# Which engine multiplies q's rows by 1/rms, in the six slots beside the first batch's MLP

## The chip, the cores and the metric

The kernel runs on one core of a Trainium2 chip. The core has a matrix engine (TensorE, PE in the profile, with its weight loads listed apart as PEld), three engines for element-wise work (VectorE = DVE, ScalarE = ACT, GpSimd = POOL), and SyncE (SP), whose queue here issues nearly all the DMAs. Every engine works its own instructions in order and waits on semaphores for the others. The metric is the device time of one execution in microseconds (us); the number quoted is the median of several executions.

## The reference

Attention with normalised q and k for 8 batches of 12 heads (448 positions, head width 64), followed by a two-layer MLP (768 to 2048 to 768) with the activation h - tanh(h):

```
q_n = q / sqrt(mean(q*q) + 1e-6) * g_q
k_n = k / sqrt(mean(k*k) + 1e-6) * g_k
attn = softmax(q_n @ k_n.T / sqrt(64))
x    = heads of (attn @ v) side by side          # (3584, 768)
h    = x @ w_in
out  = (h - tanh(h)) @ w_out
```

q, k, v are float32. The two weight matrices come as float64 and are rounded to float32 in the kernel.

## The kernel before

The attention is cut into 48 steps, one for each pair of heads of each batch (`NP` = 6 pairs, `NCH` = 4 chunks of rows, `D` = 64, `CP` = 112 rows of q in a chunk, `S` = 448). The program is written out as 51 slots, and the order of the calls in a slot is the order of the instructions on each engine: the schedule is by hand. Slots -3 to 5 (`first_slot`) hold attention alone and the first weights. Slots 6 to 11 (`early_slot`) hold attention of the second batch beside the MLP of the first; slots 12 on (`slot`) hold attention beside the MLP of the batch before. `run(gap)` puts a given amount of MLP matmuls at that place of the slot. In slots 6, 7 and 8 these are the matmuls of the first layer (line 669, 224 columns), in slots 9, 10 and 11 those of the second (line 834, 448 columns).

A step's q goes this way. Three slots ahead, `squares` (line 123) has ScalarE square q's rows into the tile `n`. `norm` (lines 133 to 135) sums them on VectorE and takes the power -1/2 on GpSimd, first for q (112x8 factors, one per row and head) and then for k. `norm_q` (line 401) multiplies q's rows by these factors, again into `n`; it is the last call of `early_slot`, after the last `run`. One slot on, `turn` (line 410) transposes k and `n` on TensorE into two PSUM banks (lines 415 and 419), and ScalarE copies them out (417, 423). There is one tile `n`, and two q tiles take turns.

The start of the next slot follows `norm_q` directly: `totals` (matmuls of line 572, whose VectorE reciprocal is line 577), then the first scores (499) with their exps on ScalarE (504). The PSUM banks named `sc` are five and go round in order: one for `totals`, four for the first scores, and `turn` takes the `totals` bank again and then the bank of the first exp.

Through slots -3 to 10 the weights are rounded. A piece is 768 KB of float64; one DMA or four bring it (lines 265, 269), then ScalarE makes two passes over it (71, 72), VectorE three (78, 79, 82, one piece behind ScalarE), and GpSimd adds the two parts (90). For all but the first eight pieces the raw data have three buffers (`w_raw`), and the next load waits on SP for the GpSimd add that frees one. Finished weights and their sums (324, 341 to 344) are written back to DRAM (332, 348), to be read again by the later batches (386, 388).

So the instructions ahead of and behind `norm_q` on VectorE in these slots are weight passes, their sums, and the additions of the MLP (725 to 739); on ScalarE the exps, the weight passes and the tanhs (705).

Of the kernel before, what the change touches and what calls it, by code (L numbers as in the profile page):

```python
# [20 lines left out]
NCH = 4  # L21
# [116 lines left out]
def bounded_path(tc, ctx, q, k, v, moe_w_in, moe_w_out, out, g_col, ident, ones, half_ones, neg_half, early):  # L138
# [17 lines left out]
    nc = tc.nc  # L156
# [3 lines left out]
    CP = S // NCH  # L160
    NP = H // 2
# [239 lines left out]
    def norm_q(s):  # L401
        rr, n = normed[s], early["n"]
        t = loaded.pop(("q", s))
        nc.vector.tensor_tensor(
            out=n.rearrange("p c h d -> p h c d"), in0=t,
            in1=rr[:CP, 1].rearrange("p (h c) -> p h c", h=2)[:, :, :, None].to_broadcast([CP, 2, NCH, D]),
            op=ALU.mult,
        )
# [470 lines left out]
    def first_slot(s):  # L879
# [21 lines left out]
        if has(s + 1):  # L901
            scores(s + 1, 2)
            add(s + 1)
            add_last(s + 1)
        norm_q(s + 3)
        if s == -3:
            early["g_col"]()
# [5 lines left out]
    def early_slot(s):  # L913
        gap = gap_ns(s)
        totals(s, sc_bank())
        if has(s + 1):
            scores(s + 1, 0)
            scores(s + 1, 1)
        if has(s + 2):
            load(s + 2, "v")  # L920
        run(gap)
        if has(s + 2):
            turn(s + 2, sc_bank(), sc_bank())
        if has(s + 3):
            squares(s + 3)
        if has(s + 4):
            load(s + 4, "qk")
        run(gap)
        if has(s + 1):
            scores(s + 1, KF)  # L930
        av = [sc_bank() for _ in range(2)]
        last_values(s, av)
        divide(s, values(s, av))
        if has(s + 1):
            scores(s + 1, 2)
        for work, n in ((add, 1), (add_last, 1), (norm, 3), (norm_q, 3)):
            run(gap / 2)
            if has(s + n):
                work(s + n)

    def slot(s):
# [50 lines left out]
        if ahead:  # L992
            norm_q(s + 3)
# [359 lines left out]
```

## Time and profile before

| | |
|---|---|
| Five runs | 1420.86 to 1427.71 us, median 1421.89 |
| The profiled execution | 1425.79 us, of which the span of the core is 1424.0 |
| Granted TensorE clock, mean | 0.989 |
| Busy share of the span | PE 97%, DVE 65%, POOL 37%, ACT 33% |

By stretches of the span (us, busy time of each engine; the six slots are about 85 to 292):

| Stretch | length | PE | DVE | ACT | POOL | clock |
|---|---|---|---|---|---|---|
| 92 to 123 | 31 | 30.37 | 30.41 | 16.58 | 18.47 | 1.00 |
| 123 to 152 | 29 | 29.00 | 26.85 | 15.58 | 16.69 | 1.00 |
| 152 to 184 | 32 | 26.13 | 25.34 | 14.95 | 13.23 | 0.84 |
| 184 to 200 | 16 | 13.70 | 15.79 | 8.67 | 12.50 | 0.98 |
| 200 to 235 | 35 | 35.00 | 29.82 | 17.02 | 18.14 | 0.96 |
| 235 to 270 | 35 | 33.81 | 31.17 | 9.59 | 15.90 | 0.95 |
| 270 to 300 | 30 | 30.00 | 19.04 | 7.98 | 6.07 | 1.00 |

A busy engine is one with an instruction begun and not ended; an instruction that is held up in the middle counts as busy all the while. Where PE is busy for less than the whole stretch it stands still for something. The clock is what TensorE was granted, 1.00 being full speed: a matmul of line 669 at half the clock takes twice as long.

### The profile page before, as it was taken

Reading aid. Unit: us, or ns where it says so; the run is one execution under the profiler, and the core shown is the slowest. Engines: PE = TensorE matmul, PEld = TensorE weight load, DVE = VectorE, ACT = ScalarE, POOL = GpSimd, SP = SyncE. Lnnn points to the kernel's source line nnn. Section 1 sums busy time; section 2 is a strip of 40 time slices with the busy share of each in tenths; the row PEclk is TensorE's granted clock in tenths of the full one; section 3 lists DMA queues with packets and bytes.
Section 4 is the critical chain, followed back from the end, with each engine's and each line's share of the span. In section 5 each row is a group of like instructions: output and inputs, shape, how many; then the busy total and the mean of one; then the engine's idle time right before and its main releaser. Section 6 shows DMA issues by size and latency. Waiting matters only on the chain.

```text
span 1424.0 us, 25566 instructions
## 1 busy us (share of the span) xinstructions
PE 1386.3 (97%) x9752; PEld 1165.8 (82%) x9752; DVE 928.0 (65%) x1571; ACT 466.8 (33%) x1070; POOL 523.8 (37%) x348
## 2 busy tenths in 40 slices
PE   6999899999999999999999999999999999999997
PEld 3568664478898799888989888987998888899997
DVE  3899879867655577567866578655875578632311
ACT  5765444233422333233332234223332333301100
POOL 4555555223521336214543145312462145401310
PEclk9999899999999999999999999999999999999999
DMA  8669788864565655665656666666556656365563
GB/s 181 165 190 245 235 247 204 219 192 149 169 169 154 166 164 176 173 171 161 178 152 186 160 162 180 172 157 167 160 174 175 171 161 179 123 180 174 187 192 95
DMA packets 355255, 249.72 MB, mean 175 GB/s; under 512 B 266484, under 2 KB 297396, under 8 KB 355124
## 3 DMA queue, kind: packets, MB, share of 16 engines
q1 hardware_dynamic: 355120, 248.00, 63.1%
q8 instruction: 79, 1.29, 0.4%
q14 instruction: 52, 0.43, 0.1%
q10 hardware_dynamic: 4, 0.00, 0.0%
HBM read 214.50 MB, written 33.42 MB: 174 GB/s over the span
## 4 chain that ended last, share of the span: by engine, by line
PE 86%; DVE 5%; DMA 3%; SPq 2%; ACT 2%; issue 1%; POOL 0%; ACTq 0%; DVEq 0%
PE mm L669 63%; PE sc L499 9%; PE sc L551 7%; PE mm L834 4%; PE sc L539 2%; SPq L265 1%; SPq L118 1%; DMA w_raw<-in_moe_w_out_dram 1%; DVE rs L577 1%; DVE w_out L82 1%; ACT sum_g L592 1%; DMA w_f<-w_in 0%; DMA gT<-in_moe_w_in_dram 0%; SPq L116 0%; DMA q_nat<-in_q_dram 0%
## 5 line engine op out<-in xcount | busy, mean ns | idle before, releaser
L669 PE MATMUL mm<-xT,w_f 128*128 128x224 f32 x1392 | 275.6, 354 | 0.0
L669 PEld LDWEIGHTS mm<-xT,w_f 128*128 128x128 f32 x1392 | 262.1, 190 | 9.1 <-issue 7.8
L669 PE MATMUL mm<-gT,w_f 128*128 128x224 f32 x1344 | 263.0, 354 | 0.0
L669 PEld LDWEIGHTS mm<-gT,w_f 128*128 128x128 f32 x1344 | 252.8, 190 | 11.4 <-issue 6.5
L457 POOL TENSOR_TENSOR rr_mine<-rr_mine,neg_half 128x28 f32<-128x28 f32 x30 | 145.1, 4835 | 251.8 <-DVE rr_mine L456 251.8
L669 PE MATMUL mm<-tt,w_f 128*128 128x224 f32 x1044 | 209.4, 354 | 5.4 <-DVE gT L706 5.4
L669 PEld LDWEIGHTS mm<-tt,w_f 128*128 128x128 f32 x1044 | 196.5, 190 | 11.4 <-DVE gT L706 7.5
L669 PE MATMUL mm<-tg,w_f 128*128 128x224 f32 x1008 | 197.7, 353 | 0.0
L706 POOL TENSOR_TENSOR gT<-s,th 128x448 f32<-128x448 f32 x96 | 115.7, 1215 | 212.7 <-ACT th L705 212.7
L669 PEld LDWEIGHTS mm<-tg,w_f 128*128 128x128 f32 x1008 | 190.6, 190 | 0.0
L499 PE MATMUL sc<-qT,kT 64*128 64x448 f32 (+1 forms) x960 | 167.4, 497 | 11.8 <-ACT p_last L504 8.3
L499 PEld LDWEIGHTS sc<-qT,kT 64*128 64x128 f32 (+1 forms) x960 | 70.1, 166 | 83.9 <-issue 60.4
L592 ACT COPY sum_g<-sum 32x14 f32<-32x14 f32 x280 | 56.3, 201 | 225.1 <-DVE sum L588 219.4
L613 DVE TENSOR_TENSOR xT<-sc,rs_T 64x224 f32<-64x224 f32 x140 | 54.4, 388 | 68.4 <-PE sc L551 66.4
L629 POOL TENSOR_TENSOR tt<-xT,tt 128x224 f32<-128x224 f32 x23 | 17.1, 744 | 222.0 <-DVE xT L613 221.9
L504 ACT ACTIVATE p<-sc 128x448 f32<-128x448 f32 x120 | 55.6, 550 | 97.9 <-PE sc L499 97.9
L705 ACT ACTIVATE th<-s 128x448 f32<-128x448 f32 x96 | 54.9, 578 | 85.0 <-DVE s L731 36.6
L135 POOL TENSOR_TENSOR rr<-rr,neg_half 112x8 f32<-112x8 f32 (+1 forms) x36 | 59.7, 1680 | 62.3 <-DVE rr L134 62.2
L551 PE MATMUL sc<-p,v_nat 128*32 128x224 f32 x1344 | 80.0, 355 | 0.0
L834 PE MATMUL mm<-gT,w_out 128*128 128x448 f32 x192 | 76.9, 557 | 0.0
L521 DVE TENSOR_TENSOR rows<-p 128x896 f32<-128x896 f32 x38 | 42.4, 1115 | 41.8 <-ACT p L504 41.7
L834 PEld LDWEIGHTS mm<-gT,w_out 128*128 128x128 f32 x192 | 36.9, 196 | 37.7 <-issue 36.3
(144 smaller groups left out, 1752.9 us busy)
## 6 DMA issues: line engine op xcount, KB each, us to landing
w_f<-w_in SPq DMA_DIRECT2D x196, 384.0 KB, 3.1
w_f<-w_out SPq DMA_DIRECT2D x147, 512.0 KB, 3.8
w_raw<-in_moe_w_out_dram SPq DMA_DIRECT2D x16, 768.0 KB, 5.1
out_dram<-th SPq DMA_DIRECT2D x192, 56.0 KB, 1.9
w_in<-w_out SPq DMA_DIRECT2D x21, 384.0 KB, 6.5
qk_nat<-in_q_dram SPq DMA_DIRECT2D x120, 56.0 KB, 2.4
qk_nat<-in_k_dram SPq DMA_DIRECT2D x120, 56.0 KB, 2.2
gT<-in_moe_w_in_dram SPq DMA_DIRECT2D x32, 192.0 KB, 4.1
```

The costliest lines, as they stand in the source:

```text
L135: nc.gpsimd.tensor_tensor(out=r, in0=r, in1=neg_half[:rows], op=ALU.pow)
L457: nc.gpsimd.tensor_tensor(out=mine, in0=mine, in1=neg_half[:, :1].to_broadcast([P, 2 * NJ]), op=ALU.pow)
L499: nc.tensor.matmul(tiles[h][i * keys : (i + 1) * keys, :n], lhsT=kT[r, c * P : c * P + keys], rhs=qT[r, i * n : (i + 1) * n], start=True, ...
L504: nc.scalar.activation(p[:, h, c if c < 2 else 0, :], tiles[h][:, :n], AF.Exp, scale=1.0 if rr is None else rr[:, 0, 2 * c + h : 2 * c + h ...
L521: nc.vector.tensor_tensor(out=t, in0=p[0], in1=p[1], op=ALU.add)
L551: nc.tensor.matmul(av[n][r : r + BL, :HS], lhsT=v_nat[:, h, c, m * BL : (m + 1) * BL], rhs=p[c][:, h, n * HS : (n + 1) * HS], start=False, ...
L592: nc.scalar.copy(out=acc[h * BL : (h + 1) * BL, g], in_=part[g * BL : (g + 1) * BL, h * NJ : (h + 1) * NJ])
L613: nc.vector.tensor_tensor(out=x[m * D : (m + 1) * D, n * HS : (n + 1) * HS], in0=av[n][m * D : (m + 1) * D, :HS], in1=rs[:, n * HS : (n + ...
L669: nc.tensor.matmul(bank[:, f * HS : (f + 1) * HS], lhsT=w[:, c * width + f, :], rhs=moving[p](c), start=(first and f == 0 and c == 0), sto ...
L705: nc.scalar.activation(th, h, AF.Tanh, bias=0.0, scale=1.0)
L706: eng.tensor_tensor(out=g[:, rows, cols], in0=h, in1=th, op=ALU.subtract)
L834: nc.tensor.matmul(bank[:, :S], lhsT=w_out_row(f, n // HC)[:, n % HC * P : (n % HC + 1) * P], rhs=g[:, f, :], start=(f == 0), stop=(f == C ...
```

## The change

`norm_q` takes another way for the steps that slots 6 to 11 prepare (steps 9 to 14). Each of the eight columns of factors (two heads by four chunks) is applied by one ScalarE instruction on 112x64 elements, with the column as its per-row scale. For all other steps VectorE does it in one instruction as before.

```diff
     def norm_q(s):
         rr, n = normed[s], early["n"]
         t = loaded.pop(("q", s))
+        if NP + 3 <= s < 2 * NP + 3:
+            for h in range(2):
+                for c in range(NCH):
+                    i = h * NCH + c
+                    nc.scalar.mul(n[:, c, h], t[:, h, c], rr[:CP, 1, i : i + 1])
+            return
         nc.vector.tensor_tensor(
             out=n.rearrange("p c h d -> p h c d"), in0=t,
             in1=rr[:CP, 1].rearrange("p (h c) -> p h c", h=2)[:, :, :, None].to_broadcast([CP, 2, NCH, D]),
```

VectorE has six instructions less, ScalarE forty-eight more. The order of everything else is the same on every engine, and the DMAs are the same.

## The prediction

> **What bounds the kernel now.** I read the chain of waits first. Its shares by engine:
>
> ```profile
> PE 86%; DVE 5%; DMA 3%; SPq 2%; ACT 2%; issue 1%; POOL 0%; ACTq 0%; DVEq 0%
> ```
>
> TensorE bounds nearly everything, so an edit on two other engines can only gain where TensorE stands still beside the six slots. The timeline of PE from 90 to 320 us has four waits of 0.6 us or more (start, duration, what; in brackets the idle time before and what ended it):
>
> ```profile
> 100.08 1.78 PE L669 MATMUL mm<-xT,w_out 128*128 128x224 f32 x8 [0.63 <-DVE s L725]
> 172.59 1.86 PE L499 MATMUL sc<-qT,kT 64*128 64x448 f32 x2 [5.87 <-ACT p_last L504]
> 199.28 1.11 PE L415 MATMUL sc<-ident,k_nat 128*128 128x128 f32 x4 [2.30 <-DVE rs L577]
> 245.59 1.02 PE L499 MATMUL sc<-qT,kT 64*128 64x448 f32 x2 [1.19 <-ACT p_last L504]
> ```
>
> The first lies before the first changed instruction (121 us). Each of the other three costs more than its idle time: in windows of one microsecond, the clock (the last column but two) is halved behind it.
>
> ```profile
> 177.00:178.00 1.00, 1.00 (x4) 0.89 (x4) 0.23 (x1) 0.00 (x0) 0.00 (x0) 0.50 1.04 418
> 179.00:180.00 1.00, 1.00 (x7) 1.00 (x6) 0.00 (x0) 0.00 (x0) 0.00 (x0) 1.00 1.02 412
> 201.00:202.00 1.00, 1.00 (x3) 0.59 (x3) 1.00 (x2) 0.89 (x3) 0.08 (x1) 0.50 1.12 334
> 249.00:250.00 1.00, 1.00 (x3) 0.44 (x2) 0.90 (x2) 0.00 (x0) 1.00 (x1) 0.50 0.73 112
> ```
>
> The same windows put the half clock at 172.6 to 178.6 (work done at half speed for 6.0 us: 3.0 lost), 199.3 to 202.6 and 247.4 to 250.7 (3.3 us each: 1.65 lost each). After the idle 0.63 it stayed at 1.00. Waits and half clock together: 5.87 + 2.30 + 1.19 + 3.0 + 1.65 + 1.65 = 15.7 us. That is all there is to win.
>
> What stands behind the longest wait, by the chain (start, us, what):
>
> ```profile
> 163.63 2.47 POOL w_out L90
> ...
> 166.12 4.37 DMA w_raw<-in_moe_w_out_dram
> ...
> 170.51 0.91 ACT w_out L71
> 171.41 0.80 ACT w_raw L72
> 172.22 0.33 ACT p_last L504
> ```
>
> A weight load could start only when GpSimd freed a raw buffer; ScalarE, in order, waited for it with the exps behind. GpSimd waited for VectorE's line 82 (162.54 to 163.50), the end of a VectorE stretch without a pause from 146.46. Line 404, the removed multiply, is in that stretch:
>
> ```profile
> 149.93 2.34 DVE L404 TENSOR_TENSOR n<-q_nat,rr 112x512 f32<-112x512 f32 x1
> 152.19 1.54 DVE L577 RECIPROCAL rs<-sc 128x224 f32<-128x224 f32 x1
> 195.74 2.02 DVE L404 TENSOR_TENSOR n<-q_nat,rr 112x512 f32<-112x512 f32 x1
> 197.68 1.55 DVE L577 RECIPROCAL rs<-sc 128x224 f32<-128x224 f32 x1
> 294.01 0.64 DVE L404 TENSOR_TENSOR n<-q_nat,rr 112x512 f32<-112x512 f32 x1
> ```
>
> Alone it takes 0.64. In the other slots GpSimd was in a two-input instruction, and line 404 ended 0.55 us after that did: add of line 90 at 149.27 to 151.71, line 404 until 152.27; 195.37 to 197.21, then 197.76; 228.36 to 230.21, then 230.76. So it was held by GpSimd. The reciprocal, which reads PSUM, takes 1.54 to 1.56 everywhere.
>
> **What is removed.** Line 404 in the six slots: 3.05 (121.11), 2.34, 2.02, 2.09 (228.67), 1.01 (262.05), 0.64, in all 11.15 us of VectorE. What each is worth:
>
> - 121.11: VectorE waits for PE at 143.56 and again at 146.46 anyway: 0.
> - 149.93: the reciprocal moves up by 2.26, and with it all behind, down to line 82 at 162.54, provided nothing there waits. The sums over PE's products (735, 731, 739 at 153.65, 157.04, 159.58) have their matmuls done at about 151.4, 153.8 and 156.1 by PE's timeline; the pieces of line 78 were loaded long before. SP is free for the load at 163.3, just before it is wanted at 163.9. So load, ScalarE's passes and exps come 2.2 us sooner: 5.87 becomes 3.7. The half clock begins as before and ends with a window; of its 3.0 between 0 and 1.8 goes, I take 0.8. Gain 3.0.
> - 195.74: the reciprocal, for which PE waits 2.30, moves up by 1.94. What is left, 0.36, is below the 0.63 that cost no clock. Gain 1.94 + 1.65 = 3.6.
> - 228.67: line 82 (233.40) and the add that frees the next buffer (234.49 to 236.54) move up 2.06, but SP is not free: it finishes v's loads at about 235.9, then writes two pieces back (0.5 each) and issues the load at about 237.2 where it was 237.79. Gain 0.55 of 1.19; the clock's 1.65 goes or stays, 0.5 for it. Gain 1.1.
> - 262.05 and 294.01: PE does not wait there: 0.
>
> Sum 7.7 us.
>
> **What is added.** Six times eight ScalarE multiplies of 112x64 with a column as scale. The trace has none of them. Nearest rows of ScalarE:
>
> ```profile
> L592 ACT COPY sum_g<-sum 32x14 f32<-32x14 f32 x280 | 56.3, 201 | 225.1 <-DVE sum L588 219.4
> L123 ACT ACTIVATE n<-q_nat 112x512 f32<-112x512 f32 x6 | 3.8, 637 | 0.0
> L417 ACT ACTIVATE kT<-sc,g_col 128x448 f32<-128x448 f32 x6 | 3.8, 628 | 11.2 <-PE sc L415 11.2
> L423 ACT COPY qT<-sc 128x448 f32<-128x448 f32 x6 | 3.1, 522 | 0.1
> ```
>
> (637 - 201) / (512 - 14) = 0.88 ns for a column; 64 columns: 201 + 50 x 0.88 = 245 ns. With a column as scale 628 against 522: 106 more, 351. Exps of 632 follow each other every 0.53 us (four in 2.21), so about 0.1 overlaps: 0.25 from one to the next. Eight: 2.0 us. Bounds: 1.8 (eight copies of line 592 take 1.78) and 2.8 (no overlap).
>
> The first of the eight waits for GpSimd's power of q (line 135, half of the pairs of 3.2 to 3.6 us). Behind it in ScalarE's queue stand four exps, for which `turn` waits by its second bank, and behind these tanhs and weight passes. By slot (us of the trace of before): the powers ready, multiplies, first exp then and now, PE's need for that bank:
>
> - 6: 120.0; 120.0 to 122.0; 119.7, 122.0; 126.2
> - 7: 146.7; 148.1 to 150.1; 149.9, 150.1; 156.4
> - 8: 191.8; 193.2 to 195.2; 193.2, 195.2; 197.8
> - 9: 226.8; 226.8 to 228.8; 226.2, 228.8; 233.4
> - 10: 260.1; 261.1 to 263.1; 262.0, 263.1; 269.2
> - 11: 289.8; 293.1 to 295.1; here the two exps of p_last are behind them, and PE needs their banks at 296.33; they end at 295.9.
>
> An exp takes 0.63, so every one is in time; `n` itself is needed where the bank is. The cover is thinnest in slot 11, 0.4 us: at 2.8 for eight, PE waits 0.4. A weight pass waits only in slot 9 (228.98 becomes 230.9, done 231.8; VectorE needs it at 232.2). I put 0.1 on all this, bounds 0 and 0.5. The load that takes over q's buffer (line 99) waits for ScalarE instead of VectorE, but is issued over 9 us later (133.95 after 122.0).
>
> Sum: 7.7 - 0.1 = 7.6. Against the profiled span: 1424.0 - 7.6 = 1416.4. The median of the runs lies 2.1 below that span: **1414.3 us**, 0.53% faster.
>
> [...]
>
> **The rivals.**
>
> *Hidden anyway.* The relief at 149.93 and 195.74 is taken up by another wait: VectorE's other two-input instructions run into GpSimd instead, or the load is bound by the DMA queue (6.98 us of write-backs at 138.48 delayed the pieces of 150). For it: those passes stretch too (line 78 took 2.24 at 164.28). Against: the reciprocal right behind is not held. It leaves one gain of 1 to 3.6 us: 1418.3 to 1420.9, say 1420.
>
> *ScalarE's queue becomes the bound.* GpSimd is late with the power (it stood behind two shrinks in slot 6 and behind the add of line 90 in slot 8), and the exps are late behind the multiplies. It decides once the power is over 3.5 us later in slot 6 (126.2 less 0.63, 2.0 and 120.0) or over 3.4 in slot 8 (power at 191.8; 197.8 less 0.63, 2.0). Price: a wait like that at 199.28, 2.30 + 1.65 = 3.95, in each, 7.9; of the gains only the 2.2 at 149.93 is left, as VectorE was not what PE waited for. 1421.9 + 5.7 = 1427.6. Against: the power depends on VectorE, which gets earlier.
>
> *More than counted*: the half clock goes at all three places and the longest wait shrinks more, 11 us or more, 1408 to 1411.
>
> That q would not move cannot be: the instruction lists have 48 more on ScalarE, six less on VectorE.
>
> **How the numbers follow.** The forecast (1411 to 1418) 0.50, hidden 0.27, ScalarE 0.15, more 0.08. The range reaches from 1409 over the hidden case to 1423. A measurement here tells 0.3% (4.3 us) from no change: below 1417.6 lie most of the forecast and all of "more" (0.54), above 1426.2 most of the ScalarE case (0.13), the rest is 0.33.
>
> **What would show it.** The wait at 172.6 down to 3.7, that at 199.3 below 0.6 with no window at 0.50 behind it, the load of 166.12 issued some 2 us earlier against the scores before it; eight multiplies in 2.0 us. Wrong would be a new PE wait on an exp of line 504 at a slot's first scores or on line 419's `n`, or the 5.87 unchanged with VectorE idle in front of line 82.

## The result and the profile after

The changed kernel takes 0.9975 of the time before, with a 95% interval of 0.9966 to 0.9983: 3.6 us less (2.4 to 4.8). The medians are 1420.38 us over 27 runs, and 1422.75 over 53 runs of the kernel before that were measured beside it; they differ by 2.4 us only, the means by 3.6, as the ratio says. The forecast was a median of 1414.3, counted from a median of 1421.89 over five runs. The kernel is faster, by less than the 0.3% that the prediction called tellable and about half of the 0.53% forecast. The profiled execution took 1423.72 us with a span of 1421.9 and a granted clock of 0.988 (before: 1425.79, 1424.0, 0.989).

Lines of the changed kernel below line 409 stand six higher than before: 499 is now 505, 577 is 583, 834 is 840; the multiplies are line 408. The shares of the chain of waits moved by a point:

```profile
PE 87%; DVE 5%; DMA 3%; ACT 2%; SPq 2%; issue 1%; POOL 0%; ACTq 0%; DVEq 0%; POOLq 0%
```

The same places in the timeline of PE (start, duration, what; in brackets the idle time before and what ended it):

```profile
101.61 1.78 PE L675 MATMUL mm<-xT,w_out 128*128 128x224 f32 x8 [0.56 <-DVE s L731]
172.17 1.86 PE L505 MATMUL sc<-qT,kT 64*128 64x448 f32 x2 [3.93 <-ACT p_last L510]
196.30 0.66 PE L421 MATMUL sc<-ident,k_nat 128*128 128x128 f32 x4 [0.38 <-DVE rs L583]
202.11 1.77 PE L840 MATMUL mm<-gT,w_out 128*128 128x448 f32 x4 [0.24 <-POOL w_out L90]
241.76 1.69 PE L505 MATMUL sc<-qT,kT 64*128 64x448 f32 x2 [1.50 <-ACT p_last L510]
```

The first line lies before any changed instruction, and this execution came there 1.53 us later than the one before (101.61 against 100.08). So I compare stretches, not points of time. From that line to the end of the first wait it needs 1.95 us less; from there to the end of the second wait 2.56 less; from there to the next scores 1.16 less (the half clock behind the second wait is gone, and about 0.5 is lost around a new short wait on a weight piece, the fourth line, of which 0.24 is idle: the 16 matmuls there take 6.63 us, where 16 take 6.11 elsewhere). Then it loses: 0.31 more to the end of the third wait and 1.65 more behind it. The sum over the six slots is 3.7 us less, as the ratio says.

The first two waits fell as forecast: 5.87 to 3.93 and 2.30 to 0.38. The third did not fall: 1.19 before, 1.50 now.

The load behind the first wait, by the chain of waits (start, us, what):

```profile
163.23 2.48 POOL w_out L90
...
165.73 4.35 DMA w_raw<-in_moe_w_out_dram
```

It stood at 166.12. Less the 1.53 that this execution was late, that is 1.92 us earlier.

The multiplies on ScalarE, in its timeline:

```profile
121.80 2.02 ACT L408 ACTIVATE n<-q_nat,rr 112x64 f32<-112x64 f32 x8 [1.10 <-POOL rr L135]
290.75 2.02 ACT L408 ACTIVATE n<-q_nat,rr 112x64 f32<-112x64 f32 x8
292.67 0.76 ACT L510 ACTIVATE p_last<-sc,rr 128x224 f32<-128x224 f32 x2
```

Eight take 2.01 to 2.03 us in every slot, for a forecast of 2.0; one takes 332 to 362 ns, median 337 (forecast 351). In slot 11, the tightest, the exps behind them end at 293.43 and PE takes up their banks at 294.15: 0.7 us to spare.

The clock behind the waits, in windows of one microsecond (the last column but two; the columns before are PE, PEld, DVE, ACT, POOL):

```profile
177.00:178.00 1.00, 1.00 (x6) 0.96 (x6) 0.62 (x1) 0.00 (x0) 0.00 (x0) 0.94 1.05 421
197.00:198.00 1.00, 1.00 (x7) 0.63 (x6) 1.00 (x1) 1.00 (x2) 1.00 (x2) 1.00 0.77 89
246.00:247.00 1.00, 1.00 (x2) 0.45 (x2) 1.00 (x1) 0.00 (x0) 1.00 (x2) 0.50 0.88 231
248.00:249.00 1.00, 1.00 (x3) 0.55 (x2) 1.00 (x2) 0.00 (x0) 0.78 (x1) 0.60 1.00 284
```

Behind the first wait the half clock ends at 177.1, 4.95 us after PE's restart where it had been 6.25. (The prediction read 6.0 there, and 3.3 behind the other two waits. The last window of each stretch, with a clock of 0.58 at 178 to 179, gives 6.25 and 3.4.) Behind the 0.38 there is none. But behind the third wait, which cost 3.4 us at half clock before, it now holds from 242.0 to 248.8, 6.8 us: 1.7 us of work more lost for a wait that is 0.3 us longer.

### The profile page after: what moved, and what is told of

Its sections match the earlier page's. It is cut to its first block, busy times and chain, and to the rows that moved or that the text cites. A ratio compares the mean times of both kernels' runs of the same rounds, so it can differ in the third digit from the quotient of the medians.

```text
span 1421.9 us, 25611 instructions
## 1 busy us (share of the span) xinstructions
PE 1387.0 (98%) x9752; PEld 1165.1 (82%) x9752; DVE 919.5 (65%) x1565; ACT 477.9 (34%) x1118; POOL 522.7 (37%) x348
## 4 chain that ended last, share of the span: by engine, by line
PE 87%; DVE 5%; DMA 3%; ACT 2%; SPq 2%; issue 1%; POOL 0%; ACTq 0%; DVEq 0%; POOLq 0%
PE mm L675 63%; PE sc L505 9%; PE sc L557 7%; PE mm L840 4%; PE sc L545 2%; DMA gT<-in_moe_w_in_dram 1%; DMA w_raw<-in_moe_w_out_dram 1%; DVE w_out L82 1%; DVE rs L583 1%; ACT sum_g L598 1%; SPq L118 1%; DMA w_f<-w_in 0%; DVE w_out L78 0%; DMA k_nat<-in_k_dram 0%; SPq L116 0%
```

## The experiments

Each was timed in five rounds beside the kernel before. The waits are those of PE in its profile, in the order above. Steps 10, 11 and 12 are those whose q is multiplied in slots 7, 8 and 9, ahead of the first, second and third wait.

| kernel | median us (runs) | ratio to before, 95% | first | second | third |
|---|---|---|---|---|---|
| before | 1422.69 to 1423.44 | 1 | 5.87 | 2.30 | 1.19 |
| changed (steps 9 to 14) | 1420.38 (27) | 0.9975 (0.9966 to 0.9983) | 3.93 | 0.38 | 1.50 |
| steps 10 and 11 only | 1420.85 (12) | 0.9982 (0.9973 to 0.9991) | 3.94 | 0.36 | 1.35 |
| step 12 only | 1424.20 (12) | 1.0005 (0.9990 to 1.0019) | 5.96 | 2.29 | 0.95 |
| step 10 only | 1423.11 (12) | 0.9988 (0.9973 to 1.0002) | 3.97 | 2.30 | 1.22 |
| step 11 only | 1423.03 (12) | 0.9993 (0.9979 to 1.0006) | 6.01 | 0.35 | 1.01 |
| changed, v late | 1416.44 (5) | 0.9948 (0.9935 to 0.9961) | 4.01 | 0.35 | none |
| before, v late | 1419.93 (12) | 0.9975 (0.9965 to 0.9986) | 5.87 | 2.30 | none |
| changed without step 12, v late | 1417.33 (5) | 0.9950 (0.9937 to 0.9963) | 3.95 | 0.36 | none |
| steps 10 and 11, v late | 1417.17 (7) | 0.9959 (0.9942 to 0.9976) | 3.97 | 0.36 | none |
| changed, each multiply twice | 1422.20 (12) | 0.9992 (0.9977 to 1.0007) | 3.90 | 0.33 | 0.77 |

**Steps 10 and 11 only.** The forecast gave the other slots' multiplies no worth, save step 12's.

```diff
-        if NP + 3 <= s < 2 * NP + 3:
+        if s in (10, 11):
```

> ScalarE multiplies only for steps 10 and 11 (slots 7 and 8); the four others stay on VectorE. Theory (the third wait, at 245.6 in before and 241.8 in the changed kernel, is set by SyncE's queue, where out stores and v's loads stand ahead of the weight load): the third wait and the half clock behind it are as in the changed kernel, 1.5 and some 3 us lost, and the time is the changed kernel's within 1 us. Rival (the multiplies of slot 9 delay ScalarE's weight passes, and so the load): the third wait falls back to 1.2 and the time is 1.5 to 2.5 us below the changed kernel.

The two steps bring 0.9982, the full change 0.9975; the intervals overlap, so the other four steps bring nothing that these runs can tell. The first two waits are those of the full change. The third wait (1.35) and the 6.8 us at half clock behind it stay too, as the theory had it and not the rival.

**One step alone.** The same line with `s == 12`, `s == 10` and `s == 11`.

> ScalarE multiplies only for step 12 (slot 9). Theory (SyncE holds the load): the third wait moves by less than 0.6 us either way, time within 1 us of before. My forecast's term for this slot: 1.1 us faster. Rival (the multiplies delay ScalarE's weight passes): 1 to 2 us slower.

> ScalarE multiplies only for step 10 (slot 7). Theory: only the first wait (5.87 at 172.6) shrinks, to about 3.9, and a little of its half clock; the second stays at 2.3 and the third at 1.2 to 1.5: 2 to 3 us below before. Rival (the gain in the first wait comes from the starting phase of that execution, not from the edit): 0.

> ScalarE multiplies only for step 11 (slot 8). Theory: the second wait falls from 2.3 to about 0.4 and its half clock goes, the first stays at 5.9: 2.5 to 3.5 us below before, less what a longer third wait takes (0 to 2). Rival (VectorE is held by GpSimd just as long in the passes that follow): the second wait stays above 1.5 and the gain is under 1 us.

In the traces each step answers for its own wait and no other. From PE's timeline, two lines with step 10 only and then two with step 11 only:

```profile
171.43 1.86 PE L505 MATMUL sc<-qT,kT 64*128 64x448 f32 x2 [3.97 <-ACT p_last L510]
198.34 0.92 PE L421 MATMUL sc<-ident,k_nat 128*128 128x128 f32 x4 [2.30 <-DVE rs L583]
171.21 1.86 PE L505 MATMUL sc<-qT,kT 64*128 64x448 f32 x2 [6.01 <-ACT p_last L510]
195.06 0.66 PE L421 MATMUL sc<-ident,k_nat 128*128 128x128 f32 x4 [0.35 <-DVE rs L583]
```

Step 10 on ScalarE takes the first from 5.87 to 3.97 and leaves the second at 2.30; step 11 takes the second to 0.35 and leaves the first at 6.01. Step 12 does nothing for the third that could be told: with it on ScalarE the third wait is 0.95 and 1.50 (0.77 with the doubled multiplies below), without it 1.19, 1.22, 1.01 and 1.35. In time the single steps bring less than I expected: 1.7 us for step 10 (expected 2 to 3) and 1.0 for step 11 (expected 2.5 to 3.5). Both intervals hold no change, and both reach into the expected range, so neither is settled; what is settled by time is the pair of them.

**The third wait: v late.** In the changed kernel GpSimd's add of line 90, which frees the raw buffer, ended at 230.41, and yet the load behind the third wait went out only at 233.67. SyncE's queue, changed kernel (SPq is the time to issue):

```profile
226.12 0.37 SPq L269 DMA_DIRECT2D w_raw<-in_moe_w_out_dram  x1
226.59 2.16 SPq L773 DMA_DIRECT2D out_dram<-th  x4
228.85 1.67 SPq L110 DMA_DIRECT2D v_nat<-in_v_dram  x1
230.56 1.84 SPq L118 DMA_DIRECT2D v_nat<-in_v_dram  x2
232.44 1.13 SPq L348 DMA_DIRECT2D w_out<-w_out  x2
233.67 0.46 SPq L269 DMA_DIRECT2D w_raw<-in_moe_w_out_dram  x1
```

SP issues without a pause from one load to the next: 7.55 us, and 7.55 in the kernel before as well. The v loads alone take 3.5 of it. The same place in the kernel before:

```profile
230.24 0.37 SPq L269 DMA_DIRECT2D w_raw<-in_moe_w_out_dram  x1
...
234.66 1.86 SPq L118 DMA_DIRECT2D v_nat<-in_v_dram  x2
236.57 1.12 SPq L348 DMA_DIRECT2D w_out<-w_out  x2
237.79 0.47 SPq L269 DMA_DIRECT2D w_raw<-in_moe_w_out_dram  x1
```

In the seven kernels with these v loads ahead, the load goes out 7.55, 7.64 and 7.28 us after the one before it with step 12 on ScalarE, and 7.55, 7.24, 7.24 and 7.21 with it on VectorE. ScalarE starts on its data 4.9 to 5.8 us after issue. The third wait goes by the sum of the two, less about 11.6: 7.55 and 5.28 give the 1.19 of the kernel before, 7.55 and 5.59 the 1.50 of the changed one, 7.28 and 5.08 the 0.77 with doubled multiplies. So its scatter is that of issuing and landing. (The chain of waits names VectorE's line 78, from 232.40 on, as this load's releaser. In the run with steps 10 and 11 alone SP's queue is as full, and that line begins only after the load, at 231.91 against 231.53, so it can't be what held it there.) So the v loads of slot 10 were moved behind its first stretch of MLP, which puts the weight load ahead of them in SP's queue:

```diff
-        if has(s + 2):
+        if s != 10:
             load(s + 2, "v")
         run(gap)
+        if s == 10:
+            load(s + 2, "v")
```

> The changed kernel, with v's load of slot 10 issued after that slot's first MLP stretch instead of before it, so that the write-backs and the weight load stand ahead of it on SyncE. Theory: the weight load is issued about 2 us earlier against the scores before it, the third wait goes and with it its half clock: 4 to 5 us below the changed kernel. Rival (ScalarE's weight passes): the load moves by less than 0.5 us, the wait stays at 1.2 to 1.5, the time within 1 us of the changed kernel.

> The kernel before, with v's load of slot 10 moved in the same way. Theory: here GpSimd's add (ending at 236.5) holds the load about as long as SyncE does, so the load moves by 0.2 us, the third wait stays near 1.1 and the time is that of before within 1 us. Rival: if SyncE alone held it in both kernels, the load moves by 2 us, the wait goes, and the time falls by 3 us or more.

> As the changed kernel with v's load moved, but step 12 (slot 9) multiplied on VectorE again. Theory: with SyncE out of the way VectorE holds the load once more; it comes 1.5 to 2 us later than with step 12 on ScalarE, and a third wait of 0.5 to 1.2 is back, with or without half clock: 0.5 to 3 us slower than the kernel with v late and all six on ScalarE. Rival (the multiply in slot 9 is of no use in any case): the same time as that kernel within 0.5 us.

The same queue with v late, changed kernel otherwise:

```profile
223.24 0.37 SPq L269 DMA_DIRECT2D w_raw<-in_moe_w_out_dram  x1
223.71 2.20 SPq L773 DMA_DIRECT2D out_dram<-th  x4
225.95 2.15 SPq L348 DMA_DIRECT2D w_out<-w_out  x2
228.20 1.33 SPq L269 DMA_DIRECT2D w_raw<-in_moe_w_out_dram  x1
```

From the start of one load's issue to the end of the next one's are 6.3 us (8.0 with v ahead), and PE's timeline has no third wait. The kernel is at 0.9948. The same move in the kernel before, with line 404 on VectorE in all slots, takes the third wait away too and gives 0.9975: the move is worth as much by itself as the whole change. There I had expected GpSimd's add to hold the load as long as SP had; it does hold it (add done at 232.69, load at 232.72), but that is 6.32 us after the last one instead of 7.55, and ScalarE starts on the data 4.57 us after issue, where it was 5.28 before. That was enough: even with 5.28 the sum would be 11.6, no wait. Nor does step 12 come to matter once SP is free, where I had expected a wait of 0.5 to 1.2 without it. The load does go out 1.4 us later without it (6.32 us after the last one, against 4.96), but no wait comes back: 0.9950 without it, 0.9948 with it.

**Steps 10 and 11 with v late.**

> Only steps 10 and 11 on ScalarE, and v's load of slot 10 moved. Theory (slots 7 and 8 are the only ones where the multiply's engine matters, and the load's place in SyncE's queue is the other half): the time of the changed kernel with v late within 1 us, that is 5.5 to 7.5 us below before; waits of about 4.0, 0.4 and none. Rival (the relief of the other four slots matters too): 1.5 us or more slower than that.

0.9959, with an interval that overlaps those of the two other versions with v late. All three beat both kernels; I can't rank them. The fastest measured is the full change with v late, 7.4 us (5.5 to 9.2) under the kernel before.

**Each multiply twice.** To see how much ScalarE's queue has to spare.

```diff
-                for c in range(NCH):
+                for c in [c for c in range(NCH) for _ in range(2)]:
```

> The changed kernel with each of the 48 ScalarE multiplies made twice in a row: 2.0 us more of ScalarE in each of the six slots, nothing else. Theory (ScalarE's cover is what I worked out from the trace): slots 6, 7, 9 and 10 hide it; in slot 8 the first exp ends about when PE needs its bank, a wait of 0 to 0.4; in slot 11 the exps of p_last end some 1.3 us after PE needs their banks, a new wait of 1 to 1.5 there. Together 1 to 3 us above the changed kernel. Rival (ScalarE's multiplies cost PE time in every slot): 2.0 in each of six, 8 to 12 us above. Other rival (ScalarE has room everywhere): within 0.7 us.

Sixteen took 5.07 us, not 4.0. Two new waits of PE appear, from its timeline:

```profile
196.00 0.60 PE L425 MATMUL sc<-ident,n 112*128 112x112 f32 x4 [0.93 <-ACT p L510]
291.39 4.55 PE L505 MATMUL sc<-qT,kT 64*128 64x448 f32 x12 [2.05 <-ACT p_last L510]
```

They are in slots 8 and 11, where the prediction had found the least cover (in 8 an exp 2.0 us ahead of its need, in 11 0.4); slots 6, 7, 9 and 10 hid even this. The 3.05 us added less the cover come near both: 3.05 - 2.0 = 1.05 in slot 8 (0.93 measured), and 3.05 - 0.7 = 2.35 in slot 11 (2.05 measured). They are longer than I expected because 3.05 us were added and not 2.0. The gain is gone as far as these runs tell: 0.9992, an interval that holds 1. So ScalarE's queue can become the bound, at 5 us for eight columns; at 2.0 it is not.

## Why the time fell by half of what was predicted

**Right: the first two waits.** "5.87 becomes 3.7" was 3.93, gain 1.94 for 2.2 (behind the reciprocal VectorE now waits 0.17 us for PE at line 741); it is 3.90 to 4.01 in all seven kernels with step 10 on ScalarE, 5.87 to 6.01 in the four without. "What is left, 0.36" was 0.38, gain 1.92 for 1.94. The way was as described: line 404 out from in front of the reciprocal, the chain behind it earlier, the load out 1.92 us earlier.

**Right: the cost.** 2.02 for eight, no wait of PE on an exp at a slot's scores or on `n`. The rival in which ScalarE's queue becomes the bound did not come, and the doubled multiplies show what it would have needed.

**Missed: 0.24.** With the second wait gone, PE reaches a weight piece 0.24 us before GpSimd has added its parts (line 90, done at 202.06), and with the restart about 0.5 goes. The prediction didn't ask what PE would wait for next there.

**Wrong: the third wait, 0.55 of the 7.6 (the 0.5 for its clock is counted with the clock below).** The step that failed is "but SP is not free: it finishes v's loads at about 235.9, then ... issues the load at about 237.2 where it was 237.79. Gain 0.55". SP was the right holder, but an SP that is busy without a pause between two loads does not finish any sooner because VectorE's line 82 did; the 7.55 us of issuing are the same in both kernels. Already the trace of before shows this, in the lines above: v's loads end there at 236.52 and not at 235.9 (234.66 plus the 1.25 that the pair takes in most slots), and from there the write-backs and the load follow at once, so SP had nothing to give. In the changed kernel GpSimd's add ended 3.26 us ahead of the load, in the kernel before 1.25, and the load came no earlier for it. Measured over the seven kernels with v ahead: no gain.

**Mis-sized: the clock, 2.95 of the 7.6.** I took the half clock as a fixed price of each wait: 1.65 at the second, 0.8 and 0.5 at the others. It is not fixed. Behind the same 2.3 of the second wait it was halved for 3.4 us in the kernel before, with step 12 only and with step 10 only, and not at all in "before, v late":

```profile
198.00:199.00 1.00, 1.00 (x5) 0.58 (x4) 0.93 (x3) 1.00 (x3) 0.00 (x0) 1.00 1.00 392
201.00:202.00 1.00, 1.00 (x4) 0.57 (x3) 1.00 (x1) 0.52 (x1) 0.85 (x1) 1.00 0.06 17
```

(PE had restarted there at 197.11; these are windows of that kernel.) Behind first waits of 3.93 to 4.01 (five profiles), PE worked at half clock for 3.4 to 6.8 us. The 0.8 at the first wait was my estimate; no run shows it for itself, nor the "between 0 and 1.8" that it was taken from. In the changed kernel's profile the 4.95 us for 6.25 are 0.65 us less lost; with steps 10 and 11 only the half clock did not begin "as before", 4.0 us ahead of the restart, but 0.6 us behind it, and held 3.4. What the profiles do show of "ends with a window" is that each half clock in them ends on the grid of 3.413 us of the last section. At the third wait 0.77, 0.95 and 1.01 cost no clock, 1.19 and 1.22 cost 3.4 us at half clock, 1.35 and 1.50 cost 6.8. In these profiles the half clock comes in steps of 3.41 us, which lie elsewhere in each (shown in the last section), and where a wait lies in the steps seems to count: the 2.30 that cost nothing was cut by a step's edge into 1.46 and 0.84, while the three that cost 3.4 us lay within one step. That is one case, and it does not explain why the price behind the third wait goes up to two steps. One profiled execution is one draw. Over all executions on record with a clock the mean granted clock is 0.9914 before (70) and 0.9921 after (29), a difference of 0.0007 with a standard error of 0.0005: 1.0 us of 1421, give or take 0.7, for the 2.95 that I had counted.

**The sum.** Idle time: 1.94 + 1.92 - 0.24 = 3.6, which is what the means give; with the mean clock's 1.0 it is 4.6. Both lie inside the interval of 2.4 to 4.8, which can't tell them apart, so that 3.6 meets 3.6 is in part luck. Of the forecast's 7.6, the third wait's idle time took 0.55 away, the clock about 2, and the smaller first gain and the new wait 0.5; the cost of 0.1 was not seen. The rival called "hidden anyway", at 1420, lies at the measured median, but by luck and not for its reason: neither of the two reliefs was taken up. Only the third was hidden.

What stays open: whether the four other steps are worth anything at all, and the worth of each of steps 10 and 11 in time. Both are below what these runs tell apart. Nor was it tried whether another place for the multiply in VectorE's own queue, clear of GpSimd's adds, would bring the same.

## What to carry to other kernels

Moving work off a busy engine pays where another engine waits for what stands behind it, and there by what the instruction takes in that place (2.02 and 2.34 us, held by a third engine, for gains of 1.92 and 1.94) and not by what it takes alone (0.64). Before counting on an earlier release, look at the queue of the one who is to use it: SP's, which issued from one transfer to the next without a pause, got there no sooner (7.55 us from load to load in both kernels), and the cure was to reorder that queue, which was worth as much here as the change itself (0.9975 each). Count idle time at its length. The half clock behind it was 0, 3.4 or 6.8 us long for waits of 0.77 to 2.30 us here, and 0 or 3.4 for the same 2.30, so count it as a mean over many runs and not from one profile.

## What the hardware showed

- **Clock.** At half clock a matmul of the changed kernel's line 675 follows the last one every 0.39 us (eight from 173.96 to 177.11), at full clock every 0.19 (36 from 177.11 to 183.93). Waits of like length had different half clocks behind them: 2.30 us none or 3.4 us, 1.01 us none, 1.22 us 3.4, 1.35 us 6.8. All changes of the clock between 92 and 300 us lie on a grid of 3.413 us within each execution. In the kernel before they are at 168.60, 178.84, 199.32, 202.74, 247.12 and 250.52 (worked out from the windows of one microsecond: a clock of 0.66 at 199 to 200 is 0.68 us at half), that is 0, 3, 9, 10, 23 and 24 steps from the first; in the changed kernel at 170.28, 177.12, 241.96 and 248.80, that is 0, 2, 21 and 23. The profiles of seven experiments (all but the doubled multiplies, and steps 10 and 11 with v late) do the same, to within 0.05 us. The grid lies elsewhere in each: PE's restart after the first wait comes 0.58 us behind the last point of it in the kernel before, 1.89 in the changed kernel, 2.78 with steps 10 and 11 only. Over 70 runs of the kernel before, time (1420.35 to 1429.09) goes with the mean granted clock at a correlation of -0.86, 0.88 us for each 0.001: most of its scatter goes with the clock. What sets the grid is not shown. How much idle time in a step halves the clock was not tested.
- **Issuing.** In slot 10, behind four stores of the result, SP took 1.67 us to issue v's first load (line 110), which takes 0.39 to 0.60 in every earlier slot and in the four that follow; with v late the two write-backs took that place, and 2.15 us where a pair takes 1.00 at 219.97 of the changed kernel, while v's load took 0.42 (changed kernel, v late). So here the slowness went with the place in the queue and not with the transfer. Four stores alone do not make it: behind those at 243.23 in the changed kernel, four write-backs took 2.13. The list of waits puts 1.0 us of line 110's issue there down to PE's transposes of `n` in both kernels (line 419 before, 425 now). What makes it is not settled.
- **Rewriting.** Eight multiplies to eight places follow each other every 0.24 us; sixteen, each place written twice running, every 0.31.
